# The signs of nine weight pieces: by products on GpSimd in place of VectorE, with a new list of first steps

## The chip, the cores and the metric

The kernel runs on one core of one Trainium2 chip. The metric is the device time of one execution in microseconds (us), and lower is better. The engines are named as in the profile: PE is TensorE, PEld its weight load, DVE is VectorE, ACT is ScalarE, POOL is GpSimd, and SP is the queue of SyncE, which issues nearly all DMAs here.

## What is computed

Inputs and weights come as numpy arrays; the four weights are float64 and q, k, v, beta are float32. B, H, S, D are 4, 8, 768, 48.

```python
k_n = k / (norm(k) + 1e-06)
for t in range(S):                      # per batch and head, state is D x D
    y[t] = q[t] @ state
    state = state + beta[t] * outer(k_n[t], v[t] - k_n[t] @ state)
x = y.transpose(0, 2, 1, 3).reshape(3072, 384)
a = x @ w1                              # 384 x 1024
b = x @ w2                              # 384 x 1024
out = ((a * b) @ w3) @ w_out            # 1024 x 1024, 1024 x 384
```

## The kernel before

**Attention in chunks.** The 768 time steps are cut into 12 chunks of 64. For a chunk, the recurrence becomes a triangular system: `scores` forms the products of keys and queries, `inverse` solves the diagonal 32x32 blocks of two chunks at once on DVE (31 steps of two instructions each, L440 and L445), `corner` fills the off-diagonal blocks with small products on PE, and `chain` and `outputs` carry the state and give y, which is copied into `xT` as the input of the second part.

**The feed-forward part.** w3 @ w_out is folded once into one 1024x384 matrix `w34` (`fold`, L759, after `transpose_w3`, L750). Then, for every pair of chunks, `ab` forms a and b (L779) and their product, and `o` multiplies by `w34` (L873).

**Pieces.** The weights arrive as float64 and are made into float32 on the chip, in 36 pieces of 128 rows by 512 (or 384) columns, by the generator `piece`. One of five `raw` buffers is filled by DMA (L699). ACT makes the magnitude from the high words (L707, Abs) and scales the low words (L708). DVE shifts the magnitude left by three bits (L710) and puts the sign bit of the high word in (L711, a `scalar_tensor_tensor` with two SBUF inputs). POOL adds the low part as integers (L715). Only then is the piece ready for PE, and only then is its `raw` buffer free for the fifth piece after it. P0 to P7 are the pieces of w_out (384 columns), P8 to P23 those of w3, P24 to P29 of w1 and P30 to P35 of w2. A piece of w1 or w2 takes four DMA issues, the others one.

**The order.** The kernel's instructions are issued in an order written out in the string `ORDER`: each name runs one generator to its next `yield`. `in_text_order` then makes every engine, and the SP queue too, keep that order. So an instruction that has to wait holds everything behind it on its own engine. In this text P14.3 is the third step of P14 (its DVE part; .1 is the DMA, .2 ACT, .4 POOL). The names used here are:

- k, q, v, p: loads of a chunk's inputs (p is a transposed load in 2 x 8 issues); g and N: squares and norms; K, Q, d: transposes of keys and queries; s: scores; u: store of the blocks to DRAM (L414).
- V0: the first inverse. V0.2 loads the blocks back (L426), V0.5 to V0.35 are the 31 steps on DVE, V0.36 and V0.37 copies on ACT (L449), V0.38 the store (L453). V1 is the next inverse.
- e: corner (e0.1 loads the blocks, L462 and L469; e0.3 is its first product, L498); c: chain; y: outputs (y.3 moves rows of xT by DMA, L684); n: scaling of v.
- t and f: transposes of w3 and folds (f2.1 and f2.2 are the two halves of fold 2; the second half needs pieces P4 to P7); a and b: products of `ab`; T: weight sums; S, o, x: sums, last product and results.

`ORDER` has 1,315 steps. The order stands for all engines together: V0's steps, for example, have the DVE steps of pieces between them.

Of the kernel before, what the change touches and what calls it, by code (L numbers as in the profile page):

```python
# [39 lines left out]
k0 P6 beta P10 P6 beta P6 P8 P6 P2 P11 K0 P10 P13 k1 P10 K0 P2 beta P11 q0 P10 P12 g0 P2 P8 P11  # L40
g0 g0 P13 K1 V0 g0 P2 P12 K0 P8 P11 K0 K0 K1 K1 P8 g0 P12 P13 g0 Q0 g0 g0 g0 Q0 Q0 P13 P18 g0
Q0 P9 Q0 K1 P12 s0 k2 P18 N0 q1 s0 K1 P7 P1 g1 s0 s0 P9 g1 Q1 Q1 Q1 Q1 P18 Q1 s0 s0 s0 P7 P18
g1 P3 P9 t2 P7 s1 s1 s1 s1 s1 s1 P7 P1 t2 P3 t5 P1 p2 d2 N0 t5 N0 P0 P0 P3 P0 u0 P9 d2 u1 P1 P3
P5 t1 P4 g1 P0 t0 V0 V0 t0 P19 t1 t10 t3 P5 t4 V0 P14 P16 f1 P5 V0 V0 V0 V0 V0 P4 P4 V0 t10 t4
f2 V0 P19 V0 t3 P14 P5 P14 P19 P17 P17 k3 s0 p2 P4 P16 V0 P17 V0 V0 V0 V0 f2 f2 f0 P17 V0 P19
P16 V0 f0 f1 P14 t11 V0 V0 f0 f1 v1 P15 P15 v0 P15 t6 t11 V0 V0 V0 V0 P16 f5 V0 P20 g1 P22 s1
P21 t8 P23 P22 t6 d2 f5 f5 P20 d2 P20 V0 P21 P15 n0 t7 P24 V0 f3 V0 t9 t8 V0 t7 t9 s2 P20 V0 n0
V0 f4 p3 n1 P22 P23 V0 V0 V0 P23 g1 d3 V0 V0 P22 g1 f3 t14 P23 f4 f3 t12 t14 P30 f4 p3 g1 V0
t15 n1 t12 P26 s1 g1 g1 f6 f7 e0 d3 N1 e0 t15 e0 P21 e1 N1 f7 e0 P21 p4 s2 d3 P24 s2 P24 e0 s2
e1 s2 e0 s2 d3 e1 P30 e1 c0 c0 f7 s3 V1 u2 P26 y0 t13 P24 P26 s3 P31 s3 P26 N1 P30 P30 y0 s3  # L50
P25 c0 P31 P25 s3 u3 s3 c0 t13 e1 c1 P31 e1 c1 P32 V1 c1 P25 V1 P28 c1 P31 V1 V1 V1 V1 V1 V1 V1
f6 V1 V1 P32 V1 V1 P32 y0 f6 V1 V1 V1 P25 P28 P28 V1 V1 v2 y1 b2 b2 b0 P32 y1 b3 b3 P27 P29 b3
b0 b0 V1 b0 b1 y1 c1 k4 a00 b1 P28 b3 P29 n2 P29 P27 P27 V1 a01 P33 a00 a00 a03 P27 V1 V1 V1 V1
a00 a02 V1 P29 V1 V1 V1 V1 a01 a03 V1 V1 b5 g2 P33 P34 a02 b5 b7 k5 a07 b2 V1 V1 P35 a06 b7 V1
b2 p4 b6 P34 g2 a06 a07 V1 n2 a04 V1 b4 b6 P33 P35 a05 g2 P34 b4 b1 c1 g2 V1 P34 a04 e2 P35 a01
P33 P35 a05 g2 a01 e3 T d4 e2 a03 c2 e2 b1 c2 e2 g2 d4 d4 g2 a04 T p5 e2 e2 d4 a05 g2 a03 a04
c2 s4 c2 g2 b5 g2 p5 a05 N2 b4 s4 s4 c2 a06 b5 c2 b4 a07 y2 d5 y2 s4 d5 T b7 s4 a02 s4 a06 b6
S0 d5 e3 v3 d5 a02 T a07 b6 S0 e3 e3 n3 V2 n3 s5 k6 g3 b7 s5 s5 S0 S0 g3 o0 c3 u4 c3 s5 N2 e3
e3 s5 S0 g3 s5 u5 x0 S0 S0 V2 o0 S0 c3 S0 c3 S0 S0 o0 x0 y3 x0 V2 V2 S0 V2 V2 V2 g3 y3 N2 o0 S0
v4 o0 c3 V2 V2 x0 V2 V2 V2 S0 V2 y3 o0 V2 S0 x0 x0 p6 V2 x0 x0 a10 V2 x0 S0 o0 V2 x0 V2 V2 a10  # L60
a16 a16 a15 a12 p6 V2 V2 a10 a11 a12 V2 k7 V2 V2 v5 g3 V2 V2 V2 a15 V2 a11 V2 a14 a17 V2 a10 x0
V2 V2 V2 d6 a12 a17 d6 g3 V2 g3 g3 e4 a14 d6 e4 a17 e4 a13 c3 c4 n5 a17 e4 a12 n4 V3 n4 g3 p7
d6 e4 g3 c4 e4 n5 a14 s6 N3 a13 s6 c4 a11 s6 a14 c4 c4 p7 y4 c4 e5 d7 a15 e5 y4 k8 e5 c5 c5 g4
d7 g4 a13 a16 e5 d7 d7 a15 a13 v6 a16 a11 s7 e5 S1 g4 g4 s7 o1 p8 s7 S1 e5 x1 s7 s7 S1 s7 c5 o1
s6 S1 u7 c5 o1 s6 s6 u6 S1 S1 V3 S1 y5 c5 c5 V3 V3 V3 V3 V3 o1 S1 x1 k9 S1 y5 S1 y5 o1 S1 S1 x1
x1 V3 S1 S1 V3 c6 V3 S1 S1 V3 d8 o1 x1 x1 v7 a20 n6 x1 V3 a20 o1 x1 a23 V3 V3 x1 V3 x1 n7 a27
a24 d8 a26 V3 V3 V3 V3 x1 g4 V3 a23 V3 a25 V3 a27 a27 V3 a24 V3 V3 a26 a20 V3 g4 V3 p8 V3 V3 V3
V3 p9 V3 V3 a25 d8 n6 d8 g4 a20 a22 a22 a24 V3 c6 a27 a25 a24 a21 a21 e6 e6 e6 g4 e7 N3 e6 a25
N3 g4 s8 g4 N4 s8 e6 a22 s8 a26 e6 c6 c6 N4 s8 a26 s8 y6 a22 V4 p9 N4 S2 d9 e7 s8 a21 e7 y6 u8
d9 a21 e7 c6 a23 d9 p10 e7 d9 S2 c6 S2 s9 n7 a23 s9 e7 o2 s9 c7 s9 S2 s9 k10 S2 c7 x2 o2 c7 S2  # L70
S2 o2 u9 s9 V4 c7 V4 S2 y7 V4 V4 x2 V4 g5 g5 V4 p10 d10 y7 S2 x2 S2 o2 y7 V4 o2 x2 c7 V4 V4 S2
S2 V4 o2 a35 x2 x2 k11 x2 S2 V4 x2 S2 a35 v8 V4 S2 V4 V4 S2 V4 x2 n8 o2 a37 x2 V4 v9 V4 V4 V4
x2 a34 n8 V4 V4 a36 a30 V4 V4 V4 V4 V4 a37 V4 a34 a33 V4 g5 a33 a30 a32 a36 V4 V4 V4 V4 a34 a33
V4 V5 a32 e8 n9 c7 e8 a30 c8 a33 e8 e9 e8 g5 a35 a34 c8 a30 e8 g5 d10 a32 e9 g5 a32 g5 a36 e8
e9 S3 c8 a36 a35 a31 d10 d10 e9 a31 n9 c8 g5 c8 c8 g5 g5 e9 a31 s10 N5 e9 p11 s10 s10 a31 c9
# [14 lines left out]
def kernel(  # L90
# [14 lines left out]
    P = 128  # L105
# [589 lines left out]
    def piece(n, srcs, dst):  # L695

        raw = in_turn(ffn, [P, CW, 2], "raw", 5, "raw", U32)
        for rows, src in srcs:
            sync.dma_start(  # L699
                out=raw[rows, 0:n].rearrange("p n w -> p (n w)"), in_=src.bitcast(U32)  # L700
            )
        yield
        dst = dst()
        lo, hi = raw[:, 0:n, 0], raw[:, 0:n, 1]
        du = dst.bitcast(U32)

        act.activation(out=dst, in_=hi.bitcast(FP32), func=ACTF.Abs, scale=2.0**-112)  # L707
        act.activation(out=lo, in_=lo, func=ACTF.Copy, scale=2.0**-29)  # L708
        yield
        dve.tensor_scalar(out=du, in0=du, scalar1=3, scalar2=None, op0=ALU.logical_shift_left)  # L710
        dve.scalar_tensor_tensor(  # L711
            out=du, in0=hi, scalar=0x80000000, in1=du, op0=ALU.bitwise_and, op1=ALU.bitwise_or
        )
        yield
        pool.tensor_tensor(out=du, in0=du, in1=lo, op=ALU.add)  # L715
        yield
# [7 lines left out]
    def piece_wo(j):  # L724
        return piece(DM, [(slice(0, P), moe_w_out[j * P : (j + 1) * P, :])], lambda: wo[:, j])

    def piece_w12(w, src, m, n0):
# [5 lines left out]
        return piece(CW, srcs, lambda: w[:, m, n0 : n0 + CW])  # L733
# [3 lines left out]
    def piece_w3(jc, hf):  # L737
        def dst():
# [4 lines left out]
            CW, [(slice(0, P), moe_w3[jc * P : (jc + 1) * P, hf * CW : (hf + 1) * CW])], dst  # L743
# [291 lines left out]
```

## Time and profile before

| | us |
|---|---|
| Median of three runs | 592.53 |
| Lowest and highest of them | 591.1 and 597.29 |
| The profiled execution, as a run | 597.89 |
| Its span in the profile | 596.2 |
| PE busy in the span | 545.3 (91%) |
| DVE busy | 363.5 (61%) |
| ACT busy | 158.8 (27%) |
| POOL busy | 176.3 (30%) |

The profiled execution was 5.4 us longer than the median of the runs. An engine's busy time is the sum of its instructions; what is not busy is idle, and the profile names what ended each idle time. The share of PE is high on the average, but the span has two parts: the first quarter, in which weights and inputs are loaded and converted, and the rest, in which PE has work at all times.

### The profile page before, as it was taken

The numbers are of one execution on the slowest core, as the hardware profiler recorded it, in microseconds if no ns is written. First come the engines' busy times: TensorE is split into PE (matmuls) and PEld (weight loads), VectorE is DVE, ScalarE is ACT, GpSimd is POOL, SyncE is SP. The second block draws the span as 40 slices with busy tenths as digits, with TensorE's granted clock in tenths as the row PEclk, the third lists the DMA queues.
The fourth block names the chain that finished last, engine by engine and source line by source line (L and its number), as shares of the span: only waits on it lengthen the run. The fifth ranks groups of instructions, "written<-read, shape, count | busy, mean of one in ns | idle before, by whom it ended". The sixth has DMA issues, their size and how long they took to land.

```text
span 596.2 us, 19061 instructions
## 1 busy us (share of the span) xinstructions
PE 545.3 (91%) x8188; PEld 381.0 (64%) x8188; DVE 363.5 (61%) x827; ACT 158.8 (27%) x333; POOL 176.3 (30%) x223
## 2 busy tenths in 40 slices
PE   2477999578999999999999989999999999999996
PEld 2465566456888884468854669645698446974476
DVE  3887997568877579665697555875746924110012
ACT  3575354353512111221210132012121112311100
POOL 7563553113355502115221034111160000600051
PEclk9998999878999899999999999999999999999999
DMA  9989986776856255553463345614333040010001
GB/s 247 186 175 266 216 155 132 129 156 120 166 81 101 70 103 93 99 92 50 110 112 73 53 70 98 130 47 72 57 65 90 13 89 4 16 46 8 1 0 53
DMA packets 219507, 57.31 MB, mean 96 GB/s; under 512 B 206656, under 2 KB 212800, under 8 KB 219424
## 3 DMA queue, kind: packets, MB, share of 16 engines
q1 hardware_dynamic: 215232, 55.31, 46.4%
q10 hardware_dynamic: 4192, 0.79, 0.9%
q8 instruction: 64, 1.05, 0.7%
q14 instruction: 19, 0.16, 0.1%
HBM read 43.88 MB, written 11.01 MB: 92 GB/s over the span
## 4 chain that ended last, share of the span: by engine, by line
PE 78%; DMA 10%; SPq 5%; DVE 3%; issue 2%; ACT 1%; POOL 1%; ACTq 0%; DVEq 0%; POOLq 0%
PE ps_f L779 41%; PE ps_f L873 19%; PE ps_w L551 5%; DMA raw<-in_moe_w_dram 4%; PE ps_w L652 4%; PE ps_f L759 3%; PE ps_w L498 3%; SPq L230 2%; PE ps_w L367 2%; PE ps_w L373 2%; DMA ktok<-in_k_dram 1%; DMA Ub<-Ud 1%; DMA Ud<-U 1%; SPq L699 1%; DMA X<-in_q_dram 1%
## 5 line engine op out<-in xcount | busy, mean ns | idle before, releaser
L779 PE MATMUL ps_f<-xT,w1s 128*128 128x512 f32 (+1 forms) x336 | 129.6, 538 | 2.6 <-DMA xT<-xT 2.6
L779 PE MATMUL ps_f<-xT,w2s 128*128 128x512 f32 (+1 forms) x336 | 131.4, 537 | 0.0
L846 POOL TENSOR_TENSOR ab<-ab 128x256 f32<-128x256 f32 x96 | 67.1, 727 | 193.6 <-DVE ab L795 167.8
L779 PEld LDWEIGHTS ps_f<-xT,w1s 128*128 128x128 f32 x336 | 64.3, 193 | 58.1 <-issue 53.7
L779 PEld LDWEIGHTS ps_f<-xT,w2s 128*128 128x128 f32 x336 | 62.2, 190 | 53.7 <-issue 50.2
L791 ACT COPY ab<-ps_f 128x512 f32<-128x512 f32 (+1 forms) x56 | 28.3, 526 | 172.3 <-PE ps_f L779 168.1
L873 PE MATMUL ps_f<-w,ab 128*128 128x192 f32 x368 | 65.0, 330 | 0.0
L795 DVE TENSOR_TENSOR ab<-ab,ps_f 128x512 f32<-128x512 f32 (+1 forms) x56 | 32.7, 603 | 48.8 <-PE ps_f L779 48.6
L873 PEld LDWEIGHTS ps_f<-w,ab 128*128 128x128 f32 x368 | 59.7, 190 | 3.9 <-issue 2.9
L440 DVE TENSOR_TENSOR tb<-Vb,Ub 128x31 f32<-128x31 f32 (+15 forms) x124 | 45.8, 370 | 14.3 <-DMA Ub<-Ud 10.9
L873 PE MATMUL ps_f<-room,ab 128*128 128x192 f32 x272 | 49.6, 337 | 0.8 <-DVE room L898 0.8
L759 PE MATMUL ps_f<-w2s,w3T 128*128 128x384 f32 x128 | 46.3, 515 | 3.4 <-POOL w2s L715 3.3
L445 DVE TENSOR_TENSOR Vb<-Vb,tb 128x31 f32<-128x31 f32 (+15 forms) x124 | 46.4, 374 | 4.3
L873 PEld LDWEIGHTS ps_f<-room,ab 128*128 128x128 f32 x272 | 45.8, 195 | 1.6 <-issue 1.1
L673 ACT COPY xT<-ps_w 48x256 f32<-48x256 f32 x96 | 30.4, 365 | 52.5 <-PE ps_w L652 52.0
L759 PEld LDWEIGHTS ps_f<-w2s,w3T 128*128 128x128 f32 x128 | 24.7, 200 | 20.3 <-POOL w2s L715 4.2
L270 POOL TENSOR_TENSOR sq<-ktok 128x384 f32<-128x384 f32 x24 | 20.6, 863 | 57.6 <-DMA ktok<-in_k_dram 27.5
L367 PE MATMUL ps_w<-KQ 48*64 48x128 f32 x384 | 30.4, 298 | 1.1 <-ACT KQ L347 1.1
L373 PE MATMUL ps_w<-KQ 48*64 48x64 f32 x768 | 30.7, 236 | 0.0
L715 POOL TENSOR_TENSOR w<-w,raw 128x512 uint32<-128x512 uint32 x16 | 20.8, 1307 | 32.2 <-DVE w L711 13.5
L537 POOL TENSOR_TENSOR vtok<-vtok,n 128x384 f32<-128x384 f32 x24 | 20.1, 849 | 33.7 <-DMA vtok<-in_v_dram 33.7
L373 PEld LDWEIGHTS ps_w<-KQ 48*64 48x64 f32 x768 | 27.8, 149 | 0.1
(110 smaller groups left out, 657.9 us busy)
## 6 DMA issues: line engine op xcount, KB each, us to landing
raw<-in_moe_w_dram SPq DMA_DIRECT2D x16, 512.0 KB, 6.9
vtok<-in_v_dram SPq DMA_DIRECT2D x24, 192.0 KB, 4.4
raw<-in_moe_w_dram SPq DMA_DIRECT2D x24, 192.0 KB, 4.3
out_dram<-osb SPq DMA_DIRECT2D x48, 96.0 KB, 2.3
ktok<-in_k_dram SPq DMA_DIRECT2D x44, 96.0 KB, 3.5
raw<-in_moe_w_out_dram SPq DMA_DIRECT2D x8, 384.0 KB, 4.7
Ud<-U SPq DMA_DIRECT2D x48, 64.0 KB, 3.3
Ub<-Ud SPq DMA_DIRECT2D x6, 512.0 KB, 3.5
```

Of the source, the lines that this page charges most:

```text
L367: pe.matmul(ps[half(z), 0, n : n + 128], lhsT=x[:, 0, :], rhs=x.rearrange("p j t -> p (j t)"), start=True, stop=True,)
L373: pe.matmul(ps[half(z ^ j), 1, n + C * j : n + C * j + C], lhsT=x[:, 0, :], rhs=x[:, j, :], start=True, stop=True,)
L440: dve.tensor_tensor(out=tv, in0=V[:, 0 : s + 1, s : s + 1].to_broadcast([P, s + 1, n]), in1=U[:, s, s + 1 : BS].unsqueeze(1).to_broadcast( ...
L445: dve.tensor_tensor(out=o, in0=o, in1=tv, op=ALU.subtract)
L551: pe.matmul(out(ps, r, h, z), lhsT=lhs(r, h, z), rhs=rhs(r, h, z), start=True, stop=True,)
L673: act.copy(out=xT[f, p:NP:2, b : b + NR, cc, :].rearrange("p a r t -> p r a t"), in_=pyv[f, z, b : b + NR],)
L759: pe.matmul(ps[:, 0:DM], lhsT=w3Ts[jc, kc // 4][:, kc % 4 * P : kc % 4 * P + P], rhs=wo[:, kc], start=(kc == 0), stop=(kc == KF - 1),)
L779: pe.matmul(ps[:].rearrange("p b c t -> p b (c t)"), lhsT=w[:, m, js], rhs=x[:, m, :, c0:c1].rearrange("p b c t -> p b (c t)"), start=(m = ...
L791: act.copy(out=t, in_=ps)
L795: dve.tensor_tensor(out=t, in0=t, in1=ps, op=ALU.mult)
L846: pool.tensor_tensor(out=o_, in0=x_, in1=y_, op=op)
L873: pe.matmul(ps[:, b, :], lhsT=abs_[u, HF * f + i][:, t0 : t0 + P], rhs=ws_[w][:, i], start=first and b == i == 0, stop=i == HF - 1 and b = ...
```

## The change

The generator `piece` gets the number of its piece. For the nine pieces in `beside` (one of w_out, eight of w3), the DVE instruction that put the sign bit in (L711) is left out. In its place ACT makes a third pass over the high words, which turns each into its sign (+1 or -1), and POOL, after the integer add, multiplies the piece by that sign in a second instruction. The other 27 pieces are converted as before.

The first 720 steps of `ORDER` are the same steps in another order; the last 595 are unchanged (they begin in the scores of chunk 7). The part of the list that the prediction speaks of is shown in the diff.

```diff
 ORDER = """
-k0 P6 beta P10 P6 beta P6 P8 P6 P2 P11 K0 P10 P13 k1 P10 K0 P2 beta P11 q0 P10 P12 g0 P2 P8 P11
-g0 g0 P13 K1 V0 g0 P2 P12 K0 P8 P11 K0 K0 K1 K1 P8 g0 P12 P13 g0 Q0 g0 g0 g0 Q0 Q0 P13 P18 g0
-Q0 P9 Q0 K1 P12 s0 k2 P18 N0 q1 s0 K1 P7 P1 g1 s0 s0 P9 g1 Q1 Q1 Q1 Q1 P18 Q1 s0 s0 s0 P7 P18
-g1 P3 P9 t2 P7 s1 s1 s1 s1 s1 s1 P7 P1 t2 P3 t5 P1 p2 d2 N0 t5 N0 P0 P0 P3 P0 u0 P9 d2 u1 P1 P3
-P5 t1 P4 g1 P0 t0 V0 V0 t0 P19 t1 t10 t3 P5 t4 V0 P14 P16 f1 P5 V0 V0 V0 V0 V0 P4 P4 V0 t10 t4
-f2 V0 P19 V0 t3 P14 P5 P14 P19 P17 P17 k3 s0 p2 P4 P16 V0 P17 V0 V0 V0 V0 f2 f2 f0 P17 V0 P19
-P16 V0 f0 f1 P14 t11 V0 V0 f0 f1 v1 P15 P15 v0 P15 t6 t11 V0 V0 V0 V0 P16 f5 V0 P20 g1 P22 s1
-P21 t8 P23 P22 t6 d2 f5 f5 P20 d2 P20 V0 P21 P15 n0 t7 P24 V0 f3 V0 t9 t8 V0 t7 t9 s2 P20 V0 n0
-V0 f4 p3 n1 P22 P23 V0 V0 V0 P23 g1 d3 V0 V0 P22 g1 f3 t14 P23 f4 f3 t12 t14 P30 f4 p3 g1 V0
-t15 n1 t12 P26 s1 g1 g1 f6 f7 e0 d3 N1 e0 t15 e0 P21 e1 N1 f7 e0 P21 p4 s2 d3 P24 s2 P24 e0 s2
-e1 s2 e0 s2 d3 e1 P30 e1 c0 c0 f7 s3 V1 u2 P26 y0 t13 P24 P26 s3 P31 s3 P26 N1 P30 P30 y0 s3
-P25 c0 P31 P25 s3 u3 s3 c0 t13 e1 c1 P31 e1 c1 P32 V1 c1 P25 V1 P28 c1 P31 V1 V1 V1 V1 V1 V1 V1
-f6 V1 V1 P32 V1 V1 P32 y0 f6 V1 V1 V1 P25 P28 P28 V1 V1 v2 y1 b2 b2 b0 P32 y1 b3 b3 P27 P29 b3
-b0 b0 V1 b0 b1 y1 c1 k4 a00 b1 P28 b3 P29 n2 P29 P27 P27 V1 a01 P33 a00 a00 a03 P27 V1 V1 V1 V1
+P0 beta k0 P8 P9 P10 g0 P0 P0 P8 beta P9 beta K0 P8 P0 P10 g0 k1 q0 K0 K1 P1 P8 P18 K0 g0 g0
+P10 P9 g0 P1 K1 t0 P2 g0 K0 K0 P18 P9 K1 Q0 g0 K1 t0 K1 P12 P2 P12 P10 P1 P1 g0 Q0 t2 t1 P2 Q0
+P13 P3 P18 P12 P2 g0 t1 q1 Q0 P18 Q0 g0 p2 N0 P3 k2 s0 t2 P7 P3 P13 P4 s0 P13 s0 P12 Q1 s0 P13
+P3 Q1 s0 s0 P5 t4 s0 Q1 Q1 Q1 g1 s1 s1 s1 u0 g1 d2 N0 g1 s1 t10 s1 V0 t4 s1 u1 P7 P4 P7 N0 P5
+P11 t10 t5 f2 P6 t5 V0 k3 f0 V0 P7 P4 V0 P11 P4 g1 P14 P6 d2 P5 P19 P5 P16 P11 V0 P6 V0 V0 f1
+V0 V0 P11 t3 V0 t3 P14 P6 f2 f2 P19 V0 P14 f0 V0 V0 V0 P15 P17 V0 P19 g1 P16 P16 V0 P14 f0 V0
+P17 v1 p2 V0 g1 V0 V0 V0 f1 P15 p3 t6 P15 P16 V0 P19 P17 v0 f5 V0 d2 V0 V0 V0 V0 f1 V0 P15 V0
+t11 d2 s1 t8 t11 P17 P20 V0 t8 s0 n1 P22 t6 f5 f5 V0 P20 P20 g1 s1 V0 P26 P23 P21 t7 t7 P20 n0
+p3 P22 P22 t9 V0 f4 V0 g1 f3 t9 V0 d3 P26 f3 t12 V0 d3 V0 P23 P22 V0 P24 P23 P23 P25 f4 f3 f4
+g1 V1 t12 g1 d3 d3 e0 P21 N1 e0 s2 t14 t15 n1 P21 t15 t14 f6 f7 e0 e1 s2 f7 p4 s2 P24 P21 P26
+P25 e0 e0 e1 n0 s2 s2 s2 N1 P26 e0 P24 c0 t13 u2 c0 e1 e1 s3 N1 y0 P27 s3 s3 P31 s3 y0 s3 u3
+P30 P25 V1 c0 P24 P27 s3 c0 P27 e1 f7 c1 e1 P25 c1 c1 t13 P31 V1 P30 P31 P32 V1 P30 V1 c1 V1 V1
+f6 y0 V1 V1 f6 y1 k4 P32 P30 V1 V1 b2 b1 V1 P32 V1 V1 P27 b3 y1 b2 P31 P28 P32 b0 V1 b1 V1 b2
+b1 b0 V1 V1 b2 P29 V1 P29 c1 b3 b1 P33 P28 P29 V1 V1 b0 b0 P28 g2 b3 y1 V1 b3 g2 V1 a03 V1 P28
...
-    def piece(n, srcs, dst):
+
+    beside = {4, 14, 15, 16, 17, 19, 20, 22, 23}
+
+    def piece(i, n, srcs, dst):
...
         act.activation(out=dst, in_=hi.bitcast(FP32), func=ACTF.Abs, scale=2.0**-112)
         act.activation(out=lo, in_=lo, func=ACTF.Copy, scale=2.0**-29)
+        if i in beside:
+            act.activation(out=hi.bitcast(FP32), in_=hi.bitcast(FP32), func=ACTF.Sign)
         yield
         dve.tensor_scalar(out=du, in0=du, scalar1=3, scalar2=None, op0=ALU.logical_shift_left)
-        dve.scalar_tensor_tensor(
-            out=du, in0=hi, scalar=0x80000000, in1=du, op0=ALU.bitwise_and, op1=ALU.bitwise_or
-        )
+        if i not in beside:
+            dve.scalar_tensor_tensor(
+                out=du, in0=hi, scalar=0x80000000, in1=du, op0=ALU.bitwise_and, op1=ALU.bitwise_or
+            )
         yield
         pool.tensor_tensor(out=du, in0=du, in1=lo, op=ALU.add)
+        if i in beside:
+            pool.tensor_tensor(out=dst, in0=dst, in1=hi.bitcast(FP32), op=ALU.mult)
         yield
```

The remaining lines of the diff hand the piece's number through `piece_wo`, `piece_w12` and `piece_w3`.

## The prediction

> **What bounds the kernel now.** I read the table of busy time by stretches first, with cuts at the start and end of the first inverse, at the first product of the corner, and at the first products of `ab`. Columns: stretch and length, then busy us and instructions of PE, PEld, DVE, ACT and POOL, PE clock, DMA share, GB/s.
>
> ```profile
> 0.00:52.10 52.10, 30.06 (x507) 25.03 (x508) 34.46 (x64) 29.55 (x54) 32.67 (x44) 0.97 0.89 216
> 52.10:85.20 33.10, 30.01 (x145) 18.09 (x144) 30.18 (x81) 15.73 (x30) 13.12 (x13) 0.95 0.95 206
> ...
> 96.20:131.40 35.20, 23.09 (x873) 18.03 (x873) 23.04 (x47) 18.32 (x35) 8.93 (x8) 0.85 0.64 120
> ...
> 143.70:300.00 156.30, 154.45 (x2724) 118.66 (x2725) 110.52 (x258) 34.99 (x81) 52.85 (x67) 0.98 0.56 100
> ```
>
> From 143.7 us on PE is full (1.9 us idle in 156), so there is nothing to win there. Before that PE idles 22 us up to 52.1 and 12 us in 96 to 131. In the stage of the first inverse three things are nearly full at once: PE (30.0 of 33.1), DVE (30.2) and the DMA engines (95%). POOL is at 40% and ACT at 48%.
>
> The chain of waits (start, length, what) shows what led from the inverse to the corner:
>
> ```profile
> 81.43 0.49 SPq L230
> ...
> 87.72 0.72 SPq L230
> 88.53 3.26 DMA Vd<-Vb
> 91.85 0.32 SPq L462
> 92.22 0.49 SPq L462
> 92.75 2.57 DMA TT<-Vd
> 95.42 0.72 DVE T L481
> 96.18 0.76 PE ps_w L498 x50
> ```
>
> The timeline has the last DVE step of V0 ending at 85.16 and its ACT copies at 86.27, but the store Vd goes out at 88.53: the SP queue was busy with the transposed loads p3 (L230). The waits of PE and DVE name two stalls more:
>
> ```profile
> PE ps_f L759 <- POOL w2s L715: 3.3, 2, 2.9
> DVE w2s L710 <- ACT w2s L707: 3.9, 1, 3.9
> PE ps_w L551 <- ACT TT L525: 4.0, 1, 4.0
> ```
>
> The first is fold 2's second half, waiting until 56.98 for w_out's last piece. The other two are one event at 114.6 to 122: P31.3 stands ahead of c1.2 in DVE's order, and its transfer landed at 117.8.
>
> **What the Trainium skill says.** "GPSIMD Engine Reference", 3.1, gives GpSimd about twice VectorE's time for an addition of two tensors (4497 against 2293 ns for 2048 columns); here 512 columns take 1.29 us on POOL (L715) and 0.69 on DVE (L711), 1.87 times, so it agrees. "SBUF — State Buffer", "SBUF: two separate sides", says that a GpSimd instruction and a DVE instruction with two SBUF inputs or in a two-port mode exclude each other for a whole instruction. The trace fits: L711 goes from 0.69 up to 1.70 us and L710 from 0.42 (384 columns: 0.35) up to 1.16, the long ones before 52 us, where POOL is 63% busy; in the stage of V0 every L710 and L711 is at its minimum, and L440 and L445, which read PSUM and one SBUF tensor there, never stretch. "ScalarE: Activation LUTs", "What ACT_TABLE_LOAD costs", says all functions cost the same per element and a switch of table set costs one load of 1283 ns; the trace has exactly one load, of 1283 ns, ahead of Abs. Its "Precision budgets" list sign with abs and relu among the cheapest functions. That it shares abs's set is likely by that page, not stated.
>
> **Part 1, DVE in the stage of V0.** Removed from DVE: L711 on nine pieces, 8 x 0.69 + 0.56 = 6.1 us. Counted in the two lists between V0.5 and V0.35: before, DVE also runs the .3 steps of P4 and seven w3 pieces (0.91 + 7 x 1.11 = 8.7), and two transposes (1.3). After, it runs P6 in full (0.91), seven shifts (7 x 0.42 = 2.9), two transposes (1.3) and two reductions (2 x 0.53 = 1.1). That is 10.0 against 6.2: **-3.8**. The 31 steps (L440 10.5 + L445 10.8) stay. Against it stands the lock: POOL's work from V0.5 to V0.35 rises from 14.4 to 23.6 us, and a shift that meets it waits. From 13 to 46 us it cost L710 some 0.2 us on the mean; I take 0.2 x 7 = **+1.4** (bounds 0, and 0.74 x 7 = +5.2 by the longest L710).
>
> **Part 2, added to ACT and POOL.** Sign: nearest row L707, 0.67 us, 9 in all; 8 of them before V0.38, +5.3 on ACT's 15.7 of 33 us. Behind it wait the copies L753 and L766 that PE needs; 12 us of ACT's idle hide it, uncovered it costs at most 5.3. Product: nearest row L393 (a float product, 1.28 us); 1.29 taken, 1.60 (longest L715) the upper bound, 1.0 for P4's 384 columns. Each such piece is ready 0.67 + 1.29 - 0.69 = 1.3 us later, and its `raw` buffer too. Behind POOL's products stand its other steps (g, n, s0, s1), and the SP queue waits for POOL where a raw buffer is needed again. I cost this at nothing on the path because the lists set the loads far enough apart; the rivals price it otherwise.
>
> **Part 3, start of V0.** In the SP queue the q1 load no longer has k2 (four issues, 3.2 us at 21.7) ahead, and the two loads ahead of V0.2 (P11, P6) reuse buffers freed long before; before, P5 waited for P9 until 44.0. The 15 pieces loaded before V0.2 are the same set and DMA is at 89%, so I take **-1.5** of a possible -3 (bounds -3, +1).
>
> **Part 4, the store of V0.** Before, p3 (2 x 8), P23, P24 and P30 crowd the queue and Vd goes 2.3 us after the copies. After, p3.1 comes earlier and only p3.2 (8 x 0.5 = 4 us) stands between P21 and Vd, beside six inverse steps. **-2.0** (0 to -2.3). Behind Vd stand eight issues (P24, P25; 8 x 0.45 = 3.6 us) ahead of the corner's loads instead of four, just over Vd's 3.3 us in flight: **+0.4**. They need P20.4 and P22.4 done on POOL.
>
> Parts 1, 3 and 4 give -3.8 + 1.4 - 1.5 - 2.0 + 0.4 = **-5.5** for the corner's loads. **But PE limits it.** I priced PE's steps by their rows (half a fold 2.75, a transpose 0.45, a product of c or scores 1.0). Both lists have 59.9 us ahead of e0.3. Before f2.2, where PE becomes full, the old list has 22.2 and the new one 25.0, because f0.1 fills what was the 2.9 us stall. If w_out's last piece comes as before, PE is ready for e0.3 2.8 us sooner; if it also comes 1.5 sooner, 4.3. I take **-3.5** at e0.3.
>
> **Part 5, from the corner to 143.7.** c1.2 now stands ahead of P31.3, so the 3.9 us stall goes. What is late next is the move of xT (y0.3), issued from 123.3 and landing about when `ab` started, 131.4. Between u3 and y0.3 the SP queue has eight raw issues and V1.2 in both lists, so I give only **-0.5** (0 to -2). Before chunk 1's `ab`, six `b` products were followed by 2.5 us of waiting for xT; now eight stand there, but y1.3 has sixteen issues (k4, P28, P29, P33) ahead where it had eight: **-0.5** (-2 to +1.5). After that PE is full and carries the shift to the end; the new order there I cost at nothing, its cover being PE's queue of ready `a` products (bounds -1, +2).
>
> Sum: -3.5 - 0.5 - 0.5 = **-4.5**: span 596.2 to 591.7, with the 1.7 us around it 593.4. That execution was 5.4 above the median; on the median, 592.5 - 4.5 = **588.0**.
>
> **Rivals.**
> **Hidden anyway.** DMA (95%) and PE (91%) stay as they are in the stage, so shorter DVE work buys nothing: 7.6 MB instead of 8.1 between V0.2 and V0.38 still need 37 us at 206 GB/s. For it: DVE was one of three. Against: PE's 2.9 us stall was a matter of order. 592.5, range 590 to 596. Chance 0.28.
> **POOL becomes the bound (slower).** From V0.21 to V0.38 POOL has 20.5 us to do in the new list (10.6 in the old), DVE 13.8, PE 19.2. In the trace this stretch lasted from 69.3 to 88.5, 19.2 us. If POOL enters it without a lead (raw loads took 5 to 8 us) it decides once its instructions average above 19.2 / 20.5 of their price; at 1.60 in place of 1.29 it takes 25.4. Then P25's buffer, and behind it e0.1, comes 6 us late, PE lacks pieces for its folds, and shifts wait on the lock (up to 3.8 more than in part 1): 592.5 + 6 + (0 to 4), with 1.5 from part 3 back, about 599, range 593 to 604. For it: L711 at 1.70 where POOL was busy. Against: POOL had 60% free, and the first half of the stage gives it a lead. Chance 0.25.
> **Sign lies in another table set (slower).** Then each of eight pieces in the stage needs two loads, 8 x 2 x 1.28 = 20.5 us on ACT, which with Signs has some 24 of 33: 45 us, 12 over, less the 4.5 gained: 600, to 604. It decides from about 3.5 pieces. Chance 0.05.
> My forecast has 0.42.
>
> **Numbers.** About 1% (5.9 us) is what can be told from no change. The likeliest case's own range is 584 to 591.5, about half of it under 586.6: faster 0.22. Slower than 598.5: half of POOL's case, the table case and some scatter, 0.22. Within 1%: 0.56. The range for 8 in 10 is 582 to 600.
>
> **What would show it.** Right: V0.5 to V0.35 near 30.7 us instead of 33.1; Vd less than 1 us behind its copies; e0.3 near 92.7; no PE wait for POOL at fold 2; DVE not waiting for P31 ahead of R (L584); one table load. Wrong: L710 at 0.8 us or more in the stage; SP (L699) waiting for POOL ahead of L462; PE waiting for POOL at L750; several table loads; new PE gaps between 143 and 300.

## The result, and the profile after

The changed kernel takes 603.95 us (median of 4 runs, 600.34 to 605.71), beside 594.23 for the kernel before (4 runs). The ratio is 1.0131, 95% interval 1.009 to 1.0172: slower by 1.3%. 588.0 was predicted, with 582 to 600 as the range, so the forecast and its range are both missed, on the side of the rivals that end slower. The profiled execution has a span of 601.6 us (603.35 as a run) against 596.2 before.

The table of busy time by stretches of the changed kernel, cut at the same events as before (start of V0.5, end of V0's last DVE step, e0.3, first `ab`, then the dense part). Columns as in the prediction's table:

```profile
0.00:54.63 54.63, 32.73 (x520) 24.93 (x521) 32.32 (x64) 30.64 (x55) 32.96 (x44) 0.91 0.86 198
54.63:87.65 33.02, 25.00 (x86) 14.40 (x85) 26.92 (x75) 18.36 (x34) 23.17 (x20) 0.96 0.96 209
100.88:135.96 35.08, 27.77 (x873) 21.32 (x873) 23.45 (x48) 14.46 (x29) 9.87 (x8) 0.71 0.65 124
143.70:300.00 156.30, 149.09 (x2767) 113.84 (x2766) 106.83 (x251) 37.12 (x85) 52.79 (x67) 0.99 0.55 94
```

Five things are to be seen. V0 begins 2.5 us later (54.63 for 52.10). Its stage is as long as before (33.02 for 33.10) although DVE is busy 3.3 us less (26.92 for 30.18): the saving is there, and is idle time. PE is busy only 25.0 us in that stage, where it was busy 30.0. From the last DVE step, which ends at 87.84 and so 0.2 us behind the cut, to e0.3 it takes 13.0 us where it took 11.0. And PE idles 7.2 us in the dense part where it idled 1.9.

The SP queue's timeline of the changed kernel (start, length of a stretch of issues, what, number of issues):

```profile
38.08 8.70 SPq L414 DMA_DIRECT2D Ud<-U  x8
...
52.63 4.77 SPq L702 DMA_DIRECT2D raw<-in_moe_w_dram  x5
57.45 1.80 SPq L213 DMA_DIRECT2D vtok<-in_v_dram  x2
59.29 9.70 SPq L230 DMA_DIRECT2D qperm<-in_q_dram  x8
69.04 4.20 SPq L230 DMA_DIRECT2D kperm<-in_k_dram  x8
73.29 1.33 SPq L213 DMA_DIRECT2D vtok<-in_v_dram  x2
74.72 6.09 SPq L702 DMA_DIRECT2D raw<-in_moe_w_dram  x8
81.90 8.56 SPq L230 DMA_DIRECT2D qperm<-in_q_dram  x8
90.56 0.43 SPq L453 DMA_DIRECT2D Vd<-Vb  x1
91.09 3.96 SPq L702 DMA_DIRECT2D raw<-in_moe_w_dram  x8
95.69 2.43 SPq L462 DMA_DIRECT2D TT<-Vd  x4
```

And lines of the same view of the kernel before:

```profile
38.19 5.75 SPq L414 DMA_DIRECT2D Ud<-U  x8
...
54.88 6.64 SPq L230 DMA_DIRECT2D qperm<-in_q_dram  x8
...
83.89 4.54 SPq L230 DMA_DIRECT2D qperm<-in_q_dram  x8
```

V0's copies on ACT, in the changed kernel and in the kernel before:

```profile
87.88 1.07 ACT L449 COPY Vb<-ps_w 128x512 f32<-128x512 f32 x2
```

```profile
85.19 1.08 ACT L449 COPY Vb<-ps_w 128x512 f32<-128x512 f32 x2 [3.68 <-DVE ps_w L445]
```

The copies end at 88.95 in the changed kernel, and its store (Vd) waits in the queue behind the eight issues of p3.2, which take 8.56 us here and took 4.54 before. Even so the store follows the copies sooner than before, after 1.6 us in place of 2.3. Behind Vd stand eight raw issues, so the corner's loads go out 5.1 us after it (3.3 before). Further up, the stores of the blocks (Ud) hold the queue for 8.70 us in place of 5.75.

The waits of the changed kernel between 52 and 91 us (engine, line, released by: us in total, times, longest):

```profile
ACT w L710 <- DMA raw<-in_moe_w_dram: 11.8, 3, 7.5
...
DVE w L715 <- ACT w L710: 4.6, 3, 2.8
```

Here is where DVE's saving went. The loads P20.1 and P22.1 stand behind p2.2 and p3.1 in the queue, ACT stands for 7.5 us at the first of them, and DVE behind ACT, in the middle of the inverse. PE, too, goes without inputs in this stage: its longest wait, 3.0 us up to 84.15, is for a copy (w3T) that stands on ACT behind that raw load. PE's waits from 54 to 91 us:

```profile
PE ps_f L767 <- ACT w3T L761: 3.2, 2, 3.0
PE ps_f L758 <- ACT w L774: 2.8, 1, 2.8
PE ps_f L758 <- POOL w L723: 1.1, 1, 1.1
PE ps_f L767 <- POOL w2s L721: 0.9, 1, 0.9
```

### The profile page after: what moved, and what is told of

Its sections match the earlier page's. It is cut to its first block, busy times and chain, and to the rows that moved or that the text cites. A ratio compares the mean times of both kernels' runs of the same rounds, so it can differ in the third digit from the quotient of the medians.

```text
span 601.6 us, 19074 instructions
## 1 busy us (share of the span) xinstructions
PE 547.1 (91%) x8188; PEld 379.8 (63%) x8188; DVE 355.1 (59%) x818; ACT 164.3 (27%) x342; POOL 188.1 (31%) x232
## 4 chain that ended last, share of the span: by engine, by line
PE 71%; DMA 11%; DVE 6%; SPq 5%; issue 3%; ACT 2%; POOL 1%; DVEq 0%; ACTq 0%; POOLq 0%
PE ps_f L787 37%; PE ps_f L881 18%; DMA raw<-in_moe_w_dram 6%; PE ps_w L551 5%; PE ps_w L652 4%; PE ps_w L498 2%; PE ps_w L367 2%; DMA ktok<-in_k_dram 2%; PE ps_w L373 2%; PE ps_f L767 1%; SPq L702 1%; SPq L230 1%; DVE tb L440 1%; DVE ps_w L445 1%; SPq L213 1%
## 5 line engine op out<-in xcount | busy, mean ns | idle before, releaser
L787 PE MATMUL ps_f<-xT,w1s 128*128 128x512 f32 (+1 forms) x336 | 127.5, 532 | 0.6 <-DVE ab L803 0.6
L767 PE MATMUL ps_f<-w2s,w3T 128*128 128x384 f32 x128 | 50.5, 550 | 4.1 <-ACT w3T L761 3.2
L881 PE MATMUL ps_f<-room,ab 128*128 128x192 f32 x272 | 48.0, 329 | 0.8 <-DVE room L906 0.8
L445 DVE TENSOR_TENSOR Vb<-Vb,tb 128x31 f32<-128x31 f32 (+15 forms) x124 | 44.5, 359 | 4.3
L881 PEld LDWEIGHTS ps_f<-room,ab 128*128 128x128 f32 x272 | 44.1, 190 | 1.7 <-issue 1.1
L767 PEld LDWEIGHTS ps_f<-w2s,w3T 128*128 128x128 f32 x128 | 26.5, 214 | 22.7 <-issue 5.3
L379 DVE TENSOR_TENSOR U<-ps_w,wt 128x512 f32<-128x512 f32 x24 | 16.5, 688 | 24.5 <-PE ps_w L373 24.3
L367 PEld LDWEIGHTS ps_w<-KQ 48*64 48x64 f32 x384 | 23.6, 143 | 10.5 <-ACT KQ L347 5.8
```

The costliest lines, as they stand in the source:

```text
L367: pe.matmul(ps[half(z), 0, n : n + 128], lhsT=x[:, 0, :], rhs=x.rearrange("p j t -> p (j t)"), start=True, stop=True,)
L445: dve.tensor_tensor(out=o, in0=o, in1=tv, op=ALU.subtract)
L767: pe.matmul(ps[:, 0:DM], lhsT=w3Ts[jc, kc // 4][:, kc % 4 * P : kc % 4 * P + P], rhs=wo[:, kc], start=(kc == 0), stop=(kc == KF - 1),)
L787: pe.matmul(ps[:].rearrange("p b c t -> p b (c t)"), lhsT=w[:, m, js], rhs=x[:, m, :, c0:c1].rearrange("p b c t -> p b (c t)"), start=(m = ...
L881: pe.matmul(ps[:, b, :], lhsT=abs_[u, HF * f + i][:, t0 : t0 + P], rhs=ws_[w][:, i], start=first and b == i == 0, stop=i == HF - 1 and b = ...
```

## The experiments

The names: "products" is the new conversion, "old list" and "new list" the two orders. All ratios are to the kernel before on the same chip. "Vd" is the start of V0's store. The new list without signs leaves the sign of nine pieces out altogether; the kernel without p3 leaves out chunk 3's transposed keys and queries. The others leave nothing out.

### The conversion or the list

Four kernels cross the two halves of the change. One is the changed kernel with the old `ORDER`; the second has the new list and no piece in `beside`; the third leaves the new list and takes both added instructions out; the fourth has the old list up to V0.5 and the new order after it.

```diff
-beside = {4, 14, 15, 16, 17, 19, 20, 22, 23}
+beside = set()                                    # new_list_vector
...
-        if i in beside:
-            act.activation(out=hi.bitcast(FP32), in_=hi.bitcast(FP32), func=ACTF.Sign)
...
-        if i in beside:
-            pool.tensor_tensor(out=dst, in0=dst, in1=hi.bitcast(FP32), op=ALU.mult)
```

> The old list of steps with the new conversion of the nine pieces. Theory A (the new list costs the time: it starts the first inverse 2.5 us later and puts raw loads P20 and P22 behind transposed loads, so that DVE waits for them): within 2 us of before, 592 to 596 when before is at 594, because DVE's saving of some 4 us in the stage of the first inverse mostly waits for SP's p3 loads and for PE. Theory B (the products and signs cost it, by POOL's longer work, later raw buffers or the lock between POOL and DVE): slower than before by 4 us or more, 598 to 606.

> The new list of steps with the old conversion of all pieces on DVE (no products, no Sign). Theory A: still slower than before, and a little slower than the changed kernel, because DVE gets 8 x 0.69 us back in the stage where the new list left no room: 602 to 610. Theory B: back near before, 592 to 598.

> The changed kernel without the third ACT pass and without the products: the nine pieces keep their magnitudes, so part of the work is left out. Theory A: the same time as the changed kernel within 2 us, 601 to 605, since the waits for P20 and P22 and the later start stay. Theory B: the added ACT and POOL work is what costs, so it falls to 594 to 598.

> The old list up to the first step of the first inverse (V0.5), then the rest in the order of the new list, with the new conversion. Theory A: V0.5 starts near 52 us as before instead of 54.6, and the 2.5 us come through to the end: 600 to 602 when the changed kernel is at 604 (the waits for P20 and P22 stay). Rival A2 (the start doesn't matter, since DMA or PE are what bound the stage after it): 603 to 605, V0.5 earlier but the corner's first product still at about 101 us.

| | ratio (95%) | V0.5 | Vd | e0.3 | first `ab` |
|---|---|---|---|---|---|
| before (profiled execution) | 1 | 52.1 | 88.5 | 96.2 | 131.4 |
| old list, products | 1.0009 (0.998 to 1.0038) | 50.7 | 86.6 | 95.0 | 128.3 |
| new list, products (the change) | 1.0131 (1.009 to 1.0172) | 54.6 | 90.6 | 100.9 | 136.0 |
| new list, VectorE's signs | 1.0137 (1.0096 to 1.0178) | 53.9 | 89.5 | 100.1 | 135.1 |
| new list, no signs | 1.0167 (1.0131 to 1.0204) | 54.5 | 89.6 | 100.3 | 134.7 |
| old list to V0.5, then new | 1.0105 (1.0058 to 1.0152) | 50.3 | 87.7 | 98.0 | 132.3 |

The conversion costs nothing and gains nothing; the list costs 1.3%, whichever conversion it carries, and even with the sign work gone. So no theory that rests on Sign, on the products or on POOL explains the result. Most of the loss comes with what follows V0.5: with the old start V0 begins 4.3 us sooner, and the run is still 1% over. Whether the start costs anything beside it can't be told from these ratios, whose intervals overlap (1.0105 and 1.0131).

### Moving single steps of the lists

If single stalls are to blame, taking them away should give time back. P24.1 and P25.1 were moved from behind Vd to behind e0.1; p3.1 behind P22.1; the list was put back to the old order from the first `ab` on; and three of the prediction's own gains were tried in the old list (P31.3 behind c1.2, p3.2 behind V0.38, P30.1 and P26.1 behind e0.1).

```diff
-V0.38 P24.1 P23.3 P23.4 P25.1 f4.2 ... e0.1 P21.2         # new_list_corner_first
+V0.38 P23.3 P23.4 f4.2 ... e0.1 P24.1 P25.1 P21.2
-P15.2 p3.1 t6.1 ... n1.1 P22.1 t6.2                       # new_list_p20_first
+P15.2 t6.1 ... n1.1 P22.1 p3.1 t6.2
```

> The changed kernel with the loads of P24 and P25 (eight issues) moved behind the corner's loads e0.1. The theory that these issues hold the corner: the loads of the corner start 3.3 us behind the store instead of 5.1, the corner's first product comes 1.5 to 2 us earlier (about 99 us) and the run is 1 to 2 us shorter than the changed kernel, 602 to 603 when that is at 604. Rival (PE has no work ready anyway, or P24 and P25 are needed at once): the first product comes earlier but the run stays at 604.

> The changed kernel with the eight transposed loads p3.1 moved behind the raw loads P20 and P22. The theory that the place in the SP queue makes P20 and P22 late: they go out at about 70 us instead of 74.7, DVE's wait of 4.4 us inside the first inverse falls under 2, the store comes 2 us earlier, the run is 1 to 2 us shorter, 602 to 603. Rival (the transfers themselves bind, the DMA engines are 96% busy in this stage whatever the order): DVE waits 3 us or more still, at P20, P22 or another piece, and the run stays within 1 us of 604.

> The new list up to the first product of ab (b2.1, 136 us), then all remaining steps in the order of the old list. The theory that a third of the loss lies in the dense part (PE idle from 143 to 300 us is 7.2 us with the new list, 2.4 with the old; ACT stands behind the transfer of P28 with copies of ab behind it): idle there falls to about 3 us and the run by 3 to 5 us, to 599 to 601. Rival (all of the loss is ahead of the corner and is only carried on): 603 to 605.

> The old list with the products, and three moves that the prediction counted as gains of the new list: p3.2 behind the store of the first inverse, P30 and P26 behind the corner's loads, and P31.3 behind c1.2. The theory that these stalls were hidden by PE's own work and by the move of xT: the store comes 2 us earlier after the inverse, DVE no longer waits 3.9 us ahead of R, and yet the run is within 1.5 us of the old list with products (594 to 596 when before is at 595). Rival (the stalls were on the path): 4 to 6 us shorter, 589 to 591.

The ratios are 1.0173 (1.0127 to 1.0219), 1.0136 (1.0088 to 1.0184), 1.0174 (1.0123 to 1.0225) and 1.0067 (1.0016 to 1.0117): no move gained. In the first, Vd's loads followed it after 3.2 us in place of 5.1, but e0.3 came only 1.3 us sooner, and PE then waited 5.2 us, until 108.3, for the loads of the second corner (L469), which now stood behind the eight raw issues. The third took on a wait of 4.6 us for xT. The second tells most. Its DVE had V0 done at 82.3, 5.6 us sooner than in the changed kernel, and DVE's wait for raw pieces in the stage was down to 0.4 us. The queue's timeline of that kernel:

```profile
71.43 8.05 SPq L230 DMA_DIRECT2D kperm<-in_k_dram  x8
79.58 2.76 SPq L702 DMA_DIRECT2D raw<-in_moe_w_dram  x6
82.44 7.11 SPq L230 DMA_DIRECT2D qperm<-in_q_dram  x8
89.64 0.43 SPq L453 DMA_DIRECT2D Vd<-Vb  x1
```

The inverse was ready at 82.3. But its copies stand on ACT behind the first steps of the piece P26, and ACT waited 3.6 us there for a raw load, until 84.83; so the copies ended at 87.0. Then the store stood behind p3.2 for 2.6 us more, until 89.64. What DVE won was lost on ACT, which waited for a load, and in the queue. In all ten kernels so far Vd came when the DMA engines had 76 to 81 us of busy time behind them (the DMA share up to Vd, times Vd; 0.89 x 90.56 = 80.6 in the changed kernel). That suggested the DMA engines as the bound.

### More and less DMA work ahead of the store

The next runs take p3 out of the new list and load it twice with the old one. Two more finish the crossing (new list up to V0.5, then the old order) and move P29.2, at which ACT stood for 3.0 us in the dense part, behind b3.2.

```diff
         for src, dst in ((k, kperm), (q, qperm)):
-            for e in range(2):
+            for e in range(0 if m == 3 else 2):           # new_list_no_p3
+            for e in (0, 1) * (2 if m == 3 else 1):       # old_list_products_p3_twice
```

> The changed kernel without the sixteen transposed loads of chunk 3 (768 KB in pieces under 512 bytes); chunk 3's transposed keys and queries are left out, all else is there. If the DMA engines set the store of V0 (about 80 us of DMA time ahead of it in every list so far; while these loads run the trace shows 50 to 130 GB/s, so 768 KB are some 7 us), Vd goes out 3 to 6 us earlier, at 84.5 to 87.5 in place of 90.56, DVE's waits for ACT at raw pieces (7.6 us in the stage) go to under 2.5, e0.3 is at 95 to 98 and the run 1 to 4 us shorter, 600 to 603. If engines or the order of DVE, ACT and POOL set it, Vd stays within 1 us of 90 (only the queue's issues go) and the run within 1 us of 604.

> The old list with products, and the sixteen transposed loads of chunk 3 issued twice: sixteen issues and 768 KB more ahead of V0's store. If the DMA engines set the store, Vd goes 4 to 7 us later than with the old list and products (86.6), at 90.5 to 93.5, e0.3 at 98 to 102, first ab 131 to 135, and the run loses 2 to 5 us (597 to 600), which would be the loss of the new list made without its order. If DMA time is hidden there, Vd stays within 2 us of 86.6 and the run within 1 us of 595.3.

> The new list up to V0.5, the steps after it in the old order; signs by products. Measured so far: V0.5 at 54.6 and first ab at 136.0 us with the new list, 50.7 and 128.3 with the old list (both by products), 50.3 and 132.3 with the old list up to V0.5 and the new one after it. If the two halves add up, here V0.5 is at 54 to 55 and the first ab 77.6 us behind it (131.5 to 133), PE idle in 143 to 300 stays near 2.5 us, and the run is 598 to 599.5, ratio 1.006. If the start of the list is what costs everything, the run is at 603. If only what comes behind V0.5 counts, because the start is caught up later, the first ab is at 129 and the run at 595.

> The changed kernel with one step moved: P29.2 (ACT's part of a piece, which waits 3.0 us for its transfer at 144.9) behind b3.2 and P28.2. If ACT's wait is what lets PE run dry at the products of ab (3.5 us of PE's 7.2 idle us in 143 to 300), PE's wait for ACT's copies there goes under 1.5 us and the run is 1 to 3 us shorter, ratio 1.008 to 1.012. If PE is short of work for another reason (xT late, T late), the wait moves to another product and the run stays at 603 to 604.

Without p3 Vd came at 83.59 (90.56 with it), the first `ab` at 126.9, and the new list's ratio fell to 1.0033 (1.0008 to 1.0057). Loaded twice, the old list's Vd came at 96.89 (86.62 once) and the run at 1.0148 (1.0095 to 1.0201), the loss of the changed kernel without its list. So what stands ahead of Vd in the queue moves the run both ways. The stage of V0 in the kernel without p3:

```profile
53.60:82.30 28.70, 23.77 (x86) 13.95 (x85) 26.95 (x75) 18.70 (x34) 21.86 (x19) 1.00 0.95 226
```

DVE's busy time is that of the changed kernel (26.95 and 26.92), and now the stage is only 1.75 us longer than it. With the queue out of the way the saving on DVE does shorten the inverse, and the store follows V0's copies at once (they end at 83.56).

The halves did not add up: the new list up to V0.5 with the old order behind it gave 1.0147 (1.0094 to 1.0199), Vd at 96.15. The joint puts steps together that neither list had together (the SP queue waited 11.9 us for POOL at raw buffers), so this crossing says nothing of either half. P29.2's move gave 1.0164 (1.012 to 1.0208): PE's wait for ACT's `ab` copies was gone from the dense part, and others stood in its place.

### The queue or the DMA engines

Each of p3's sixteen loads is 512 packets and one issue. Two runs part them. The first adds sixteen issues with 32 packets each (1% more packets), the second leaves the packets and lets ACT issue them. Three others move p3, with the DVE transposes d3 that read it, behind the corner's loads.

```diff
+            if m == 3:                                    # old_list_products_small_issues
+                ... sync.dma_start(out=dst[...][:, 0:1], in_=src[e, 0:1, ...])
             for e in range(2):
...
-                        sync.dma_start(                   # before_p3_on_act
+                        (act if m == 3 else sync).dma_start(
...
-f4.1 p3.1 ... g1.6 d3.1 ... p3.2 ... e0.1 d3.2 ... e1.1 ... p4.1 ... d3.3 ... d3.4 ... s3.1
+f4.1 ... g1.6 ... e0.1 ... e1.1 p3.1 p3.2 ... d3.1 d3.2 d3.3 d3.4 p4.1 s3.1   # p3_behind_V0, old list
```

> The old list with products, and sixteen more issues ahead of p3's own, each with 32 packets in place of 512: in all 512 packets more (1% of the 40,900 ahead of V0's store) and 8 us of the SP queue's time at 0.49 us an issue. If the DMA engines' time is what counts, Vd comes within 1.5 us of 86.6 (85.5 to 88.1) and the run within 1.5 us of the kernel before. If the queue's time for issues is what counts, Vd comes 6 to 10 us later (93 to 97), as with the full loads issued twice (96.9), and the run at 1.010 to 1.015.

> The kernel before with p3's sixteen loads issued by ACT (idle for 17 of 33 us in the stage) in place of the SP queue: the same packets at much the same time, and 8 us less of the SP queue's time. If the DMA engines' time counts, Vd stays at 86.5 to 89 and the run within 0.3% of the kernel before. If the queue's time counts, Vd comes directly behind V0's copies, 2 to 4 us earlier, at 84 to 86, and the run 2 to 4 us shorter, ratio 0.993 to 0.997.

> The old list with products; the sixteen transposed loads of chunk 3 (p3) go behind the corner's loads (e0.1, e1.1), and the DVE transposes that read them (d3), with p4's first half, directly ahead of chunk 3's scores. Nothing is left out. If DMA time ahead of V0's store sets the corner and the corner sets the run, Vd goes out 3 to 6 us earlier than 86.6 (80.5 to 83.5), the first ab comes at 122 to 126, and the run is 3 to 6 us under the kernel before, ratio 0.990 to 0.995. If the work only comes back later (DVE waits for p3 ahead of chunk 3's scores, or the second inverse starts later), the first ab comes early but the run stays within 2 us of the kernel before.

> The kernel before (signs by VectorE, old list) with the same move of p3, d3 and p4's first half. If the conversion is neutral wherever DMA time sets the stage, it is within 0.3% of the run with products; if with the DMA time gone DVE's time in the inverse decides, the products' version is 2 to 4 us the faster of the two.

> The changed kernel with the same move. If DMA time ahead of V0's store is the mechanism of its loss too, Vd comes at 83 to 87 in place of 90.6, the first ab at 127 to 132, and the run is 4 to 8 us under the changed kernel (596 to 600, ratio 1.000 to 1.006). If the loss lies in the order behind the first ab, the run is at 602 to 604 in spite of an earlier first ab.

| | issues ahead of Vd | Vd | DMA share to Vd | ratio |
|---|---|---|---|---|
| old list, products | 93 | 86.6 | 0.93 | 1.0009 |
| with 16 small issues | 109 | 95.3 | 0.84 | 1.0121 (1.0061 to 1.0182) |
| with p3 twice | 109 | 96.9 | 0.92 | 1.0148 |
| the changed kernel | 89 | 90.6 | 0.89 | 1.0131 |
| without p3 | 73 | 83.6 | 0.89 | 1.0033 |

The reading with 80 us of DMA time fell. Sixteen issues that move next to nothing put Vd 8.6 us later, nearly as far as the full loads did (10.3), while the DMA engines' share went down to 0.84 and their busy time up to Vd stayed what it was (0.84 x 95.25 = 80.0). The SP queue's timeline of that kernel (its lines are 14 further down: L231 are the small issues, L244 p3's own):

```profile
76.53 4.59 SPq L231 DMA_DIRECT2D kperm<-in_k_dram  x8
81.17 4.15 SPq L244 DMA_DIRECT2D kperm<-in_k_dram  x8
85.41 1.82 SPq L716 DMA_DIRECT2D raw<-in_moe_w_dram  x4
87.33 3.62 SPq L231 DMA_DIRECT2D qperm<-in_q_dram  x8
91.05 4.09 SPq L244 DMA_DIRECT2D qperm<-in_q_dram  x8
95.25 0.43 SPq L467 DMA_DIRECT2D Vd<-Vb  x1
```

V0's last step was at 84.12 there, and its store 11 us behind, with issue upon issue ahead of it. The small issues and p3's own take 0.45 to 0.57 us each in these lines; that, and not the bytes, is what stood ahead of Vd. The skill's "DMA: Bandwidth & Descriptors", "Issuing engines are not separate DMA queues", says that issuing from several engines saves only the sequencer's time, "which is usually small relative to the DMA itself". Here it is not small: one of p3's loads is some 0.54 us of the DMA engines' time (an estimate: (0.92 x 96.89 - 0.93 x 86.62) / 16), and its issue takes as long. In these two kernels the queue's issues hold the store and the store holds PE, which waited 9.1 us (p3 twice) and 7.1 us (small issues) ahead of e0.3. In the changed kernel PE waited 1.8 us there, and fewer issues stand ahead of Vd than in the old list (89 for 93). So the price of an issue is shown, but the count of issues ahead of the store does not by itself explain the changed kernel's loss.

Giving the issues to ACT did not help. Vd came at 87.29, 1.2 us sooner, but ACT too is held by what it issues. The chain of waits of that kernel:

```profile
88.53 4.33 DMA qperm<-in_q_dram
92.86 0.02 issue
92.88 2.40 DMA raw<-in_moe_w_dram
95.27 0.59 ACT w3T L753
95.86 0.04 issue
95.90 8.11 PE ps_f L759 x16
```

The eight issues of p3.2 lie on ACT from 88.53 to 95.2, the copies that PE's folds need behind them, PE waits 6.3 us, and e0.3 is at 103.9: ratio 1.009 (1.0058 to 1.0123).

Moving p3 behind the corner brought Vd to 84.4 (old list, products), 84.9 (old list, VectorE's signs) and 83.6 (new list), and no run: 1.0078 (1.0049 to 1.0108), 1.0087 (1.0058 to 1.0115), 1.0176 (1.0122 to 1.023). The loads were missed at chunk 3's scores. The wait of PE in the corner's stage of the first of them:

```profile
PE ps_w L367 <- DVE KQ L324: 5.0, 1, 5.0
```

It is 7.1 us in the second and 10.7 in the third. So p3 cannot simply go later. Nor did the earlier store help at the corner of the first two: PE came to e0.3 from its own work, with no wait for the corner's loads, at 94.99 in the first (95.02 with p3 in its old place) and at 94.18 in the second.

```profile
94.99 0.76 PE L498 MATMUL ps_w<-T,U 33*33 33x32 f32 x64
```

These runs also show once more what the conversion does on its own. With the queue out of the way, V0's stage took 30.4 us with products and 33.2 with VectorE's signs:

```profile
52.68:83.10 30.42, 28.36 (x145) 17.04 (x144) 25.55 (x72) 21.12 (x40) 23.27 (x20) 1.00 0.93 228
```

```profile
50.38:83.55 33.17, 30.51 (x151) 18.44 (x150) 29.95 (x80) 16.78 (x32) 14.57 (x14) 1.00 0.88 208
```

(The first fence is the old list with products, the second the kernel before, both with p3 moved.) The gain that the change was made of is real, 2.8 us in these two executions, but the two kernels take the same time: PE, and then the loads of p3, set what follows. (That V0 started 2.3 us later in the first is within the scatter of single executions, as the sum below shows.)

The last run moves two raw loads ahead of the block stores, which hold the queue from 38.1 to 46.8 in the new list.

```diff
-s1.3 u0.1 ... P5.2 P11.1 t10.2 t5.1 f2.1 P6.1 t5.2 V0.2    # new_list_raw_before_U
+s1.3 P11.1 P6.1 u0.1 ... P5.2 t10.2 t5.1 f2.1 t5.2 V0.2
```

> The changed kernel with two steps moved: the loads P11.1 and P6.1 ahead of the stores of the blocks (u0.1), which wait in the queue for chunk 0's and 1's scores from 38.1 to 46.8 us while the DMA engines fall to 0.72. If queue order there is what costs the new list its DMA time, the share in 38 to 47 goes to 0.85 or more, Vd comes 1.5 to 3 us earlier (87.5 to 89) and the run 1 to 3 us. If the loads have no free buffer then (they wait for POOL), the stores are held instead and V0 starts later than 54.6, run 604 or more.

It filled the hole (DMA share in 38 to 47 us 0.87 for 0.72) and V0 started at 52.4, 2.2 us sooner in this execution. But Vd stayed at 91.0 and the run at 1.0134 (1.0086 to 1.0183): ACT stood 8.9 us at one raw piece in the stage.

## Why the prediction was wrong, by its own steps

**Part 1, DVE in the stage: right, but without effect.** DVE's busy time in the stage fell by 3.3 us against -2.4 forecast, and the lock's price was met: L715 took 603 ns on the mean there, where L710 took 421, so 7 x 0.18 = 1.3 us against +1.4. The step that failed is that the stage would shorten to 30.7. It stayed at 33.0, because DVE waited 4.6 us for raw pieces that the queue brought late. That is no fault of the new list alone: in the old list with products, whose stage took 32.2, DVE waited as long from 52 to 91 us:

```profile
DVE w L715 <- ACT w L710: 4.8, 3, 2.9
```

Where p3 went behind the corner the stage was 30.4, and with P20 and P22 ahead of p3.1 it was 29.2, with DVE waiting 0.4 us for a piece and a DMA share of 0.88. The text had this as a rival, "hidden anyway", with the DMA engines and PE as the cover. What covered the saving was the place of the raw loads in the SP queue.

**Part 2, Sign and product at nothing: right.** Sign took 0.67 us, the product 1.30, one table load was seen, and old list with products is 1.0009. Both slower rivals that rested on it fell: POOL was busy 23.2 of 33.0 us, with instructions at 1.29 to 1.36 us and not 1.60. One sign of the POOL rival did show, PE waiting for products (1.1 us, and its weight load PEld 4.7); but without any product the new list is as slow (1.0137).

**Part 3, start of V0: wrong in sign.** -1.5 was forecast with +1 as the bound, and it was +2.5 (+2.3 on the mean of all lists with either start, as the sum shows). I compared the raw loads ahead of V0.2 and not the chain that releases the block stores. In the new list three Q1 copies stand on ACT behind chunk 0's last PT copy. Chunk 1's scores wait for them, and its last U (L379) ran at 44.12, where it ran at 40.35 before. The stores in the queue waited for it, with P11 and P6 behind them.

**Part 4, the store: right ahead of Vd in sign, at a third of the size; wrong behind it.** The queue was forecast to give 2.0 us and gave 0.7 (1.6 us from the copies to Vd for 2.3). The term that was mis-sized is "p3.2 (8 x 0.5 = 4 us)", which took 8.56. Five raw issues (and two of v) stand directly ahead of p2.2 and eight ahead of p3.2 in the new list, and these transposed issues took 1.21 and 1.07 us each (9.70 / 8 and 8.56 / 8). In the old list with products, p3.2 took 0.51 (4.08 / 8). The queue's wait for raw transfers at L230 was 3.7 us up to Vd. That Vd came 2.0 us later than before comes of the later start and of a stage as long as before: 2.5 + 0.2 - 0.7. The eight issues behind it cost 1.8 (5.1 for 3.3), not 0.4.

**"But PE limits it": wrong, and the sum took its term from here.** -3.5 was forecast for e0.3, with PE full from f2.2 on. e0.3 came 4.7 us later (100.88 for 96.18). PE did not become full: between V0.5 and e0.3 it idled 9.8 us where it had idled 3.7. It stood 8.0 us for copies on ACT and pieces on POOL, the longest time behind the raw load at which ACT stood (the waits shown above), and at the end 1.8 us for the corner's loads:

```profile
100.88 0.76 PE L498 MATMUL ps_w<-T,U 33*33 33x32 f32 x64 [1.78 <-DVE T L481]
```

**Part 5, corner to the dense part: wrong.** The stall at c1.2 did go, as said. Yet from e0.3 to the first `ab` it took 35.08 us against 35.20 (-1.0 was forecast up to 143.7). In the two tables the same 873 matmuls are busy 27.77 us where they were 23.09, at a granted clock of 0.71 for 0.85: what the stall had cost came back as slower matmuls. That is not the new order's alone: in the old list with products, which keeps the old order there, they are busy 25.86 us at 0.74. Behind the first `ab` the new order was costed at nothing, bounds -1 and +2. From the first `ab` to the end, nine kernels with the old order there took 462.8 to 466.2 us (mean 464.4) and ten with the new one 465.6 to 470.2 (mean 467.4), with the same matmuls to do: 3.0 us more (the kernel put back to the old order from there on is in neither group; it took 473). PE's waits in the dense part of the changed kernel:

```profile
PE ps_w L498 <- issue: 1.9, 1, 1.9
PE ps_f L787 <- ACT ab L799: 1.5, 1, 1.5
PE ps_w L498 <- DVE T L481: 1.4, 1, 1.4
PE ps_w L367 <- DVE PT L397: 0.9, 1, 0.9
```

**The sum.** Against the old list with products, whose profiled execution (593.2) is nearer to its median than that of the kernel before, the changed kernel loses 3.9 us up to V0.5, nothing from there to Vd, 1.9 from Vd to the corner's loads, nothing to e0.3, 1.8 to the first `ab`, and 0.7 after it: 8.4 in all, 593.2 to 601.6. A pair of single executions does not fix these shares. The nine profiled kernels with the old list up to V0.5 start V0 between 50.3 and 52.7 us (mean 51.5), and the ten with the new list up to there between 52.9 and 54.6 (mean 53.8). On the means of the executions whose order is the same up to the point in question, the new list loses 2.3 us up to V0.5, 2.6 from there to e0.3 (two kernels against five), 0.4 to the first `ab`, and 3.0 after it (the nine and the ten kernels of part 5): 8.3 in all. -4.5 was forecast.

**What stays open.** Which steps of the new order cost the 3 us behind the first `ab` wasn't found; moving P29.2 only changed the wait's name. That p2.2 and p3.2 take longer behind bursts of raw loads is read from the timeline; no run parted the bursts, and since the queue's wait there is for raw transfers, the DMA engines may bind at that place. And no version was found that beats the kernel before: the best, old list with products, equals it.

## What to carry to other kernels

Count the issues of the DMA queue as work of an engine: time each, in order, and ask what the store that all wait for stands behind. In a stage where three engines are nearly full, work taken off one of them comes back as a wait unless its inputs come sooner too (here the stage was 33.0 us long until loads were moved, then 29.2). A list that was balanced by hand answered nearly every moved stall with another one here, so price a new order by following the releases (who frees the store, who frees that) and not by counting instructions between two names. A high DMA share beside a late transfer is no proof that bytes are the bound: add issues without bytes to find out.

## What was not expected of the hardware

Matmuls of one form (128x384, L767) took 486 ns or 1007 ns in the stretch from 95 to 131 us of the changed kernel (median 486; the numbers after the count are the lowest, the median and the highest in ns):

```profile
L767 PE MATMUL ps_f<-w2s,w3T x25: 486/486/1007, 94.7 to 130.9; 128*128 128x384 f32 x25
```

The skill's "TensorE: Matmul & The Clock Gate", "What's actually happening", has PE at half its clock until it has been busy for about 3.4 us, and says that the window in which this is judged runs freely. The trace agrees with the two durations (a ratio of 2.07). The granted clock was near 0.50 from 102.4 to 105.8 and from 116.0 to 133.1 us in the changed kernel, and from 116.0 to 126.3 in the kernel before: 3.4, 17.1 and 10.2 us, which are one, five and three times 3.4. The full clock came back 3.9 us after PE's last gap in the kernel before (its end is at 122.4), and 6.3 us after it in the changed kernel (126.8). So a gap ahead of PE can cost more than its length. The wait of 1.8 us at e0.3 was followed by eight of these matmuls that took 4.54 us, where they had taken 2.85. And the sum of PE's gaps does not tell the clock: in the corner's stage PE idled 12.1 us before and 7.3 after, at 0.85 and 0.71.
